# Experts' activations laid out by pairs, fixed tiles, and a new written order for the start of a convolution and gated feed-forward kernel

## The chip, the cores and the metric

The kernel runs on one core of a Trainium2 chip. The metric is the device time of one execution in microseconds (us). TensorE (PE) multiplies matrices, VectorE (DVE) and ScalarE (ACT) work elementwise, GpSimd (POOL) works elementwise and issues the adding DMAs, SyncE (SP) issues the plain DMAs.

## The reference

Sixteen thousand positions (4 sequences of 4160, width 192) pass through two stages.

```
w   = softmax(weight_gen, axis=-1)            # 8 heads x 7 taps a position
y   = sum over k of w[s, head, k] * x[s-6+k]  # each head has 24 of the 192 columns
h   = relu(y @ w_in)                          # 192 -> 1024
c   = conv_w[0]*h[s-1] + conv_w[1]*h[s] + conv_w[2]*h[s+1]
out = (h * sigmoid(c)) @ w_out                # 1024 -> 192
```

## The kernel before

**Tiling.** Each of the 128 partitions holds 130 consecutive positions. They are worked in 33 blocks of 4 positions (R = 4, so 512 columns a block once transposed). Block 0 gives 2 output positions, later ones 4, since the three-tap convolution lags by its edge.

**One block.** POOL multiplies 7 shifted copies of the ring of x with the softmax weights (`tap`, line 324). From block 3 on, two adding DMAs issued by POOL (`fold1`, line 347, and `fold2`, line 350) and one POOL addition (`fold3`, line 357) sum them; in blocks 0 to 2 PE sums them while it transposes (`transposes`, line 372). ACT and DVE split the transposed result into a high and a low part (`split_hi`, 392, `split_lo`, 396). Then follow 8 units, one for each 128 of the 1024 hidden columns (called experts here): `mm1` (5 matmuls, line 410) into one of 5 PSUM tiles z, `relu` (416) from z to h, `wmid` (420) from h to z, two `conv_side` (427), `sig` (434) and `gmul` (472). In blocks 2 to 31 the products of experts 0 and 1 are split once more (`g_hi` 457, `g_lo` 460). `mm2` (493) gives 4 output tiles of 16 matmuls, ACT copies them out (500), POOL adds two halves (506), SP stores (510).

**The carry.** h holds for each expert 6 rows of 128: rows 2 to 5 are the block's, rows 0 and 1 are the last two of the block before. `carry` (line 477) copies rows 4 and 5 to rows 0 and 1 for two experts with one DMA on SP's queue; `relu` of the next block waits for it. In the old layout `h[partition, expert, row, 128]` the two rows of one expert are one piece of 1,024 bytes, so a carry has two pieces a partition.

**Weights.** w_in, conv_w and w_out arrive as 64-bit numbers and are decoded on ACT and DVE in chunks at the start: `shift_exp` (165), `low` (168), `clamp` (172), `shift` (175), `sign` (178), `add` (183), then a split into high and low (687, 692). The chunks of w_in are f0 and f1 (the folded last 64 rows, spread by DMAs from line 706) and m0, m1, m2; conv_w is transposed on PE (658) and read back by ACT (664).

**The order.** Every step is a task with a number, an engine, a duration and its inputs. The instructions are written out in the order of the list `ORDER`, then, for the tasks that are not in it, in the order of a planner that places tasks by these durations and by the arrival times `T_X`, `T_W`, `T_CW` and those in `CH`. Each engine and each DMA queue runs its own instructions strictly in that order. Numbers that are used below: 4 to 11 softmax group 0 (maximum, subtract, exp, sum, epsilon, reciprocal, zero, normalise), 13 to 20 group 1, 22 to 28 group 2, 30 to 36 group 3; 38 to 45 conv_w; 47 to 56 chunk f0, 58 to 65 m0, 67 to 76 f1, 78 to 85 m1, 87 to 94 m2; 129 to 135 the taps k = 0, 1, 2, 4, 5, 6, 3 of block 0, 136 to 153 its transposes and splits, 156 to 162 the taps of block 1; 183 the first `mm1`; 204, 220, 229, 245 the carries of block 0; 288, 304, 320, 336 those of block 1; 338, 435, 536, 638, 740 the loads of x for blocks 3 to 7; 745 the subtract of softmax group 4.

`PLAN` names the engine of each tap of blocks 0 to 2 (V is DVE, G is POOL), in the order k = 0, 1, 2, 3 and then 4, 5, 6 (index i is tap k = i). `SMX` names the engines of a softmax group's subtract and normalise. Where a tap, a subtract or a normalise with both inputs in SBUF runs on DVE (the planner's "VK"), the next POOL instruction in written order is preceded by a token: DVE clears a small tile (`tok`, line 988), and POOL writes it (989), so POOL waits until DVE has come to that place.

**Tiles.** Before, w, the softmax sums, the tap products (px, py), the split inputs and z come from pools that hand out a buffer at each request.

## Time and profile before

| | |
|---|---|
| median of 3 runs | 696.84 us (696.56 to 697.0) |
| profiled execution | 696.19 us, its span 694.5 us |
| PE busy | 674.3 us, 97% of the span |
| DVE busy | 654.7 us, 94% |
| ACT busy | 598.5 us, 86% |
| POOL busy | 570.7 us, 82% |

The span runs from the first to the last instruction of the program in the profile; 1.7 us of the execution lie around it. Busy shares are means over the whole span: the start, in which the weights are decoded and the first blocks are made, and the end differ from the steady part.

### The profile page before, as it was taken

How to read it: one execution, taken by the hardware profiler on the slowest of the kernel's cores; microseconds unless marked ns; L12 is line 12 of the kernel's file. 1: busy time of each engine (PE TensorE's matmuls, PEld its weight loads, DVE VectorE, ACT ScalarE, POOL GpSimd, SP SyncE). 2: the span in 40 equal slices, each digit the busy share in tenths (PEclk: the TensorE clock that was granted, in tenths of full speed). 3: DMA queues.
4: the chain of work that ended last, by engine and by line, in shares of the span. 5: the costliest groups of instructions: out<-in, count | busy, mean ns of one | idle time of the engine just before them, and what ended most of it. 6: DMA issues, size and time to landing. Idle time of an engine off the chain costs nothing.

```text
span 694.5 us, 11226 instructions
## 1 busy us (share of the span) xinstructions
PE 674.3 (97%) x3749; PEld 612.6 (88%) x3749; DVE 654.7 (94%) x1061; ACT 598.5 (86%) x1147; POOL 570.7 (82%) x451
## 2 busy tenths in 40 slices
PE   2999999999999999999999999999999999999998
PEld 2788988999999999999999999999999999999997
DVE  6999998999999999999999999999999999999991
ACT  3778888989898998989899998989899898888982
POOL 5999998899998988989797997989799897971111
PEclk9999999999999999999999999999999999999999
DMA  8627889999899887889788787888878788692211
GB/s 267 205 77 156 216 203 228 211 217 217 201 213 209 176 204 185 210 199 214 198 197 199 174 207 197 205 208 197 202 148 210 179 209 180 159 203 87 83 54 46
DMA packets 70785, 127.61 MB, mean 184 GB/s; under 512 B 5054, under 2 KB 42557, under 8 KB 70728
## 3 DMA queue, kind: packets, MB, share of 16 engines
q0 software_dynamic: 20192, 59.01, 47.1%
q1 hardware_dynamic: 50188, 67.42, 29.2%
q8 instruction: 30, 0.49, 0.3%
q10 hardware_dynamic: 348, 0.47, 0.2%
q14 instruction: 27, 0.22, 0.1%
HBM read 20.51 MB, written 12.78 MB: 48 GB/s over the span
## 4 chain that ended last, share of the span: by engine, by line
PE 84%; POOL 11%; issue 2%; DMA 1%; ACT 1%; DVE 0%; POOLq 0%; ACTq 0%
PE ops L493 43%; PE z L410 38%; POOL px L324 5%; POOL py L324 4%; PE tp L372 3%; DMA h<-h 1%; PE z L493 1%; POOL w L298 0%; POOL w L276 0%; POOL px L350 0%; POOL px L347 0%; POOL px L357 0%; ACT h L416 0%; DVE z L427 0%; ACT z L420 0%
## 5 line engine op out<-in xcount | busy, mean ns | idle before, releaser
L427 DVE SCALAR_TENSOR_TENSOR z<-h,cw,z 128x512 f32<-128x512 f32 (+1 forms) x528 | 376.1, 741 | 8.1 <-ACT z L420 4.4
L410 PE MATMUL z<-H,wi 128*128 128x512 f32 x1056 | 299.1, 404 | 1.9 <-DVE g L472 1.2
L493 PE MATMUL ops<-wo,g 128*128 128x192 f32 x1536 | 273.3, 328 | 0.0
L493 PEld LDWEIGHTS ops<-wo,g 128*128 128x128 f32 x1536 | 246.7, 190 | 0.0
L324 POOL TENSOR_TENSOR px<-ring,w 128x768 f32<-128x768 f32 (+2 forms) x146 | 232.7, 1703 | 1.1
L410 PEld LDWEIGHTS z<-H,wi 128*128 128x128 f32 x1056 | 194.6, 188 | 39.7 <-DVE g L472 2.9
L420 ACT ACTIVATE z<-h,cw 128x512 f32<-128x512 f32 (+1 forms) x264 | 180.0, 682 | 4.8
L324 POOL TENSOR_TENSOR py<-ring,w 128x768 f32<-128x768 f32 (+3 forms) x109 | 170.4, 1912 | 0.0
L434 ACT ACTIVATE z<-z 128x512 f32<-128x512 f32 (+1 forms) x264 | 151.6, 576 | 19.3 <-DVE z L427 14.7
L416 ACT ACTIVATE h<-z 128x512 f32<-128x512 f32 x264 | 155.9, 591 | 10.1 <-PE z L410 7.9
L472 DVE SCALAR_TENSOR_TENSOR g<-z,h 128x512 f32<-128x512 f32 (+1 forms) x198 | 130.6, 675 | 1.2
L506 POOL TENSOR_TENSOR o<-o 128x768 f32<-128x768 f32 x30 | 68.0, 2268 | 48.2 <-ACT o L500 30.9
L410 PE MATMUL z<-L,wi 128*128 128x512 f32 x264 | 103.1, 390 | 0.0
L493 PE MATMUL ops<-wos,gx 128*128 128x384 f32 x480 | 90.5, 310 | 0.5 <-ACT o L500 0.5
L500 ACT ACTIVATE o<-ops 128x384 f32<-128x384 f32 (+1 forms) x128 | 61.5, 483 | 25.6 <-PE ops L493 25.0
L493 PEld LDWEIGHTS ops<-wos,gx 128*128 128x128 f32 x480 | 74.8, 189 | 6.1 <-ACT o L500 0.9
L357 POOL TENSOR_TENSOR px<-px 128x512 f32<-128x512 f32 (+1 forms) x60 | 72.8, 1460 | 3.8 <-DMA px<-px 3.8
L410 PEld LDWEIGHTS z<-L,wi 128*128 128x128 f32 x264 | 49.6, 188 | 11.1
L392 ACT ACTIVATE H<-tp 64x256 fp32r<-64x256 f32 (+1 forms) x93 | 42.5, 458 | 8.7 <-PE tp L372 8.3
L350 POOL DMA_DIRECT2D px<-px x30 | 40.0, 1335 | 11.5 <-DMA px<-py 11.1
L347 POOL DMA_DIRECT2D px<-py x30 | 39.6, 1320 | 9.4 <-POOL py L324 8.2
L472 DVE SCALAR_TENSOR_TENSOR z<-z,h 128x512 f32<-128x512 f32 x60 | 41.7, 695 | 1.3 <-ACT z L434 0.2
(77 smaller groups left out, 384.0 us busy)
## 6 DMA issues: line engine op xcount, KB each, us to landing
px<-py POOLq DMA_DIRECT2D x30, 1152.0 KB, 8.8
h<-h SPq DMA_DIRECT2D x128, 256.0 KB, 4.4
px<-px POOLq DMA_DIRECT2D x30, 768.0 KB, 6.6
ring<-in_x_dram SPq DMA_DIRECT2D x31, 384.0 KB, 5.6
out_dram<-o SPq DMA_DIRECT2D x31, 384.0 KB, 5.7
w<-in_weight_gen_dram SPq DMA_DIRECT2D x15, 224.0 KB, 4.8
r_out<-in_moe_w_out_dram SPq DMA_DIRECT2D x4, 384.0 KB, 4.5
wi<-scr SPq DMA_DIRECT2D x8, 128.0 KB, 3.1
```

The lines of the kernel that those rows point to most:

```text
L324: eng.tensor_tensor(out=dst[:, a:b, :].rearrange("p s (h g) -> p s h g", g=GRP), in0=ring[:, p:p + n, :].rearrange("p s (h g) -> p s h g", ...
L357: nc.gpsimd.tensor_tensor(out=dst.rearrange("p (s d) -> p s d", s=R), in0=a[:, :, lo:hi], in1=b[:, :, lo:hi], op=ALU.add)
L392: nc.scalar.activation(out=hi, in_=src, func=ACTF.Copy)
L410: nc.tensor.matmul(out=z, lhsT=w[:, fs], rhs=h_t[j, nm], start=(i == 0), stop=(i == len(terms) - 1))
L416: nc.scalar.activation(out=hrow(f, 2, R), in_=z_t[j, f], func=ACTF.Relu)
L420: nc.scalar.activation(out=z_t[j, f][:, :no * P], in_=hrow(f, cc, no), func=ACTF.Copy, scale=cw[:, NF + f:NF + f + 1])
L427: nc.vector.scalar_tensor_tensor(out=z, in0=hrow(f, cc + d, no), scalar=cw[:, k * NF + f:k * NF + f + 1], in1=z, op0=ALU.mult, op1=ALU.add,)
L434: nc.scalar.activation(out=z, in_=z, func=ACTF.Tanh, scale=0.5)
L472: nc.vector.scalar_tensor_tensor(out=g_of(j, f), in0=z_t[j, f][:, :no * P], scalar=1.0, in1=hrow(f, cc, no), op0=ALU.add, op1=ALU.mult)
L493: nc.tensor.matmul(out=ps[:, 0:m], lhsT=g, rhs=w, start=(n == 0), stop=(n == len(terms) - 1))
L500: nc.scalar.activation(out=o_t[j][:, 0:n, i, :], in_=ps[:, 0:n * D].rearrange("p (b d) -> p b d", b=n), func=ACTF.Copy, scale=0.5)
L506: eng.tensor_tensor(out=o[:, 0, a:b], in0=o[:, 0, a:b], in1=o[:, 1, a:b], op=ALU.add)
```

## The change

The layout of h becomes `[partition, pair, row, expert of the pair, 128]`. One expert's row is still 128 numbers in a run, but its rows now stand 256 numbers apart, so `relu`, `wmid`, `conv_side` and `gmul` address h as 4 runs of 128. A carry's two rows of two experts are now one piece of 2,048 bytes a partition.

The pools of w, the softmax sums, px, py, the split inputs and z become fixed tiles, as many as before, taken in turn by block or unit number (conv_w takes z tile 0, the units follow from tile 1). The softmax of group 0 subtracts on POOL, that of group 1 subtracts on POOL and normalises on DVE; tap k = 6 of block 0 moves to DVE. The planner's arrival times change, the ring's reuse distance in its model changes from 3 to 4 blocks (`RB`), and `ORDER` is new and has 700 entries instead of 600. The loads at the start are issued as before.

```diff
-    ("a", "GVGGGGG"),
+    ("a", "GVGGGGV"),
...
-SMX = ("VG", "VV", "GG", "GG")
+SMX = ("GG", "GV", "GG", "GG")
...
-T_CW = 3.7
-T_X = (9.0, 12.8, 14.6)
-T_W = (4.2, 11.1, 20.1, 21.1)
+T_CW = 5.0
+T_X = (8.8, 11.0, 12.4)
+T_W = (3.2, 10.0, 16.0, 17.1)
...
-    ("f", 0, 256, 5.3, "VGP", "G"),
-    ("m", 0, 256, 10.1, "VVP", "G"),
-    ("f", 256, 512, 15.7, "GVP", "V"),
-    ("m", 256, 512, 16.8, "VVP", "G"),
-    ("m", 512, 1024, 19.1, "VVP", "V"),
+    ("f", 0, 256, 6.3, "VGP", "G"),
+    ("m", 0, 256, 9.4, "VVP", "G"),
+    ("f", 256, 512, 13.3, "GVP", "V"),
+    ("m", 256, 512, 14.0, "VVP", "G"),
+    ("m", 512, 1024, 15.3, "VVP", "V"),
...
-    "38 40 4 5 47 6 41 39 7 9 49 50 8 10 11 129 42 48 51 52 131 53 130 43 133 132 54 58 44 60 61 59 45 136 137 139 "
-    "141 134 138 13 62 135 140 14 15 142 144 63 64 65 67 16 17 69 70 68 71 72 55 73 74 75 95 18 143 19 78 80 20 156 "
...
+    "38 39 4 5 6 7 9 10 47 8 11 129 49 132 50 40 41 51 131 48 52 53 133 42 54 58 60 61 62 137 59 63 13 14 43 44 64 65 "
+    "68 45 136 55 130 139 67 69 70 71 72 73 22 74 78 75 79 23 135 134 80 15 16 18 81 82 141 143 17 19 83 84 145 138 "
+    "20 338 156 140 142 85 147 144 146 151 148 161 30 152 153 164 149 150 183 157 87 89 90 91 24 163 190 95 197 158 "
...
-    RB = (RING - R - TAPS) // R
+    RB = (RING - R - 2) // R
...
-    h = const.tile([P, NF, R + 2, P], F32, name="h")
+    h = const.tile([P, NF // CG, R + 2, CG, P], F32, name="h")
...
+    px_b = [const.tile([P, 4, R, D], F32, name=f"px{i}") for i in range(NX)]
+    py_b = [const.tile([P, 3, R, D], F32, name=f"py{i}") for i in range(NY)]
+    t_b = [[const.tile([P, W], F32R, name=f"{t}_{i}") for t in ("H1", "L1", "H2")] for i in range(2)]
+    z_b = [ps_z.tile([P, W], F32, name=f"z{i}") for i in range(NZ)]
...
-        z = ps_z.tile([P, W], F32, tag="z", name="z")
-        z_t[j, f] = z
+        z = z_t[j, f] = z_b[(1 + j * NF + (f if j else FORD.index(f))) % NZ]
...
     def hrow(f, a, n):
-        return h[:, f, a:a + n, :].rearrange("p s t -> p (s t)")
+        return h[:, f // CG, a:a + n, f % CG, :]
...
     def carry(f0):
-        nc.sync.dma_start(out=h[:, f0:f0 + CG, 0:2, :], in_=h[:, f0:f0 + CG, R:R + 2, :])
+        nc.sync.dma_start(
+            out=h[:, f0 // CG, 0:2].rearrange("p s f t -> p (s f t)"),
+            in_=h[:, f0 // CG, R:R + 2].rearrange("p s f t -> p (s f t)"),
+        )
```

## Rows read from the trace of the kernel before

**Rows 1.** Windows: stretch, then each engine's busy us and instructions, PE clock, DMA share

```profile
300.00:400.00 100.00, 100.00 (x556) 91.44 (x555) 97.78 (x155) 90.26 (x170) 89.46 (x68) 1.00 0.84 197
```

**Rows 2.** Timeline of PE: start, us, line, operands, count, idle before and its releaser

```profile
23.68 1.17 PE L410 MATMUL z<-H,wi 128*128 128x512 f32 x4
...
29.78 0.96 PE L410 MATMUL z<-H,wi 128*128 128x512 f32 x3 [0.24 <-DVE wi L692]
...
40.29 0.73 PE L410 MATMUL z<-H,wi 128*128 128x512 f32 x2 [0.16 <-DVE H L396]
...
52.26 1.19 PE L410 MATMUL z<-H,wi 128*128 128x512 f32 x4 [0.24 <-DVE gx L472]
...
93.68 0.39 PE L410 MATMUL z<-L,wi 128*128 128x512 f32 x1
94.54 0.81 PE L493 MATMUL ops<-wos,gx 128*128 128x384 f32 x4 [0.47 <-ACT o L500]
...
116.17 0.39 PE L410 MATMUL z<-L,wi 128*128 128x512 f32 x1
117.79 1.21 PE L410 MATMUL z<-H,wi 128*128 128x512 f32 x4 [1.23 <-DVE g L472]
```

**Rows 3.** The chain that ended last, 85 to 150 us: start, us, what

```profile
88.77 0.94 POOL w L276
...
104.88 10.07 DMA h<-h
...
144.44 5.68 PE z L410 x25
```

**Rows 4.** Timeline of POOL

```profile
9.66 1.54 POOL L324 TENSOR_TENSOR px<-ring,w 128x768 f32<-128x768 f32 x1
11.16 2.25 POOL L324 TENSOR_TENSOR px<-ring,w 128x768 f32<-128x768 f32 x1
...
21.58 0.10 POOL L989 MEMSET tok<- 128x1 f32 x1 [1.74 <-DVE tok L988]
...
26.18 0.97 POOL L276 TENSOR_TENSOR w<-w,m 128x448 f32<-128x448 f32 x1
...
62.05 1.54 POOL L324 TENSOR_TENSOR px<-ring,w 128x768 f32<-128x768 f32 x1
```

**Rows 5.** Timeline of SP's queue

```profile
2.54 0.58 SPq L207 DMA_DIRECT2D ring<-in_x_dram  x1
```

**Rows 6.** DMA issues from 0 to 4 us: operands, queue, count, KB, us to landing

```profile
ring<-in_x_dram SPq DMA_DIRECT2D x1, 588.0 KB, 6.2
```

**Rows 7.** Timeline of DVE

```profile
7.61 0.43 DVE L172 TENSOR_SCALAR dps<-dps 128x256 f32<-128x256 f32 x1
...
9.78 2.24 DVE L324 TENSOR_TENSOR px<-ring,w 128x768 f32<-128x768 f32 x1
...
14.69 0.75 DVE L276 TENSOR_TENSOR w<-w,m 128x448 f32<-128x448 f32 x1
...
16.36 0.42 DVE L692 TENSOR_TENSOR wi<-dps,wi 128x256 fp32r<-128x256 f32 x1 [0.57 <-ACT wi L687]
...
22.21 0.68 DVE L396 TENSOR_TENSOR L<-tp,H 128x512 fp32r<-128x512 f32 x1
...
24.32 1.14 DVE L273 TENSOR_REDUCE m<-w 128x64 f32<-128x448 f32 x2
```

**Rows 8.** Timeline of ACT

```profile
6.36 0.40 ACT L165 ACTIVATE dps<-stage 128x256 f32<-128x256 f32 x1 [1.18 <-DMA stage<-in_moe_w_in_dram]
...
66.49 0.58 ACT L416 ACTIVATE h<-z 128x512 f32<-128x512 f32 x1
```

**Rows 9.** The page's DMA queues: packets, MB, share of 16 engines' span

```profile
q0 software_dynamic: 20192, 59.01, 47.1%
q1 hardware_dynamic: 50188, 67.42, 29.2%
```

**Rows 10.** Groups of instructions by shape: count, busy us, mean ns, idle before

```profile
L396 DVE TENSOR_TENSOR H<-tp,H 64x256 fp32r<-64x256 f32 x60 | 25.4, 423 | 7.3 <-ACT H L392 6.3
```

More of the change, by code (lines that the diff above doesn't have):

```diff
@@ L271, in vmax @@
         def vmax():
-            sm_t[j] = [sm_p.tile([P, 2 * R * HEADS, 1], F32, tag=t, name=t) for t in ("m", "r")]
+            sm_t[j] = sm_b[j % 2]
             V.tensor_reduce(out=m(0)[:, :, 0], in_=w(), axis=AX.X, op=ALU.max)
@@ L412, in hrow, with rows @@
     def hrow(f, a, n):
-        return h[:, f, a:a + n, :].rearrange("p s t -> p (s t)")
+        return h[:, f // CG, a:a + n, f % CG, :]
+    def rows(ap):
+        return ap.rearrange("p (s t) -> p s t", t=P)
     def relu(j, f):
-        nc.scalar.activation(out=hrow(f, 2, R), in_=z_t[j, f], func=ACTF.Relu)
+        nc.scalar.activation(out=hrow(f, 2, R), in_=rows(z_t[j, f]), func=ACTF.Relu)
     def wmid(j, f):
@@ L420, in wmid @@
         nc.scalar.activation(
-            out=z_t[j, f][:, :no * P], in_=hrow(f, cc, no), func=ACTF.Copy, scale=cw[:, NF + f:NF + f + 1]
+            out=rows(z_t[j, f][:, :no * P]), in_=hrow(f, cc, no), func=ACTF.Copy, scale=cw[:, NF + f:NF + f + 1]
         )
@@ L425, in conv_side @@
         no, cc = geom(j)
-        z = z_t[j, f][:, :no * P]
+        z = rows(z_t[j, f][:, :no * P])
         nc.vector.scalar_tensor_tensor(
@@ L472, in gmul @@
         nc.vector.scalar_tensor_tensor(
-            out=g_of(j, f), in0=z_t[j, f][:, :no * P], scalar=1.0, in1=hrow(f, cc, no), op0=ALU.add, op1=ALU.mult
+            out=rows(g_of(j, f)), in0=rows(z_t[j, f][:, :no * P]), scalar=1.0, in1=hrow(f, cc, no), op0=ALU.add, op1=ALU.mult
         )
     def carry(f0):
-        nc.sync.dma_start(out=h[:, f0:f0 + CG, 0:2, :], in_=h[:, f0:f0 + CG, R:R + 2, :])
+        nc.sync.dma_start(
+            out=h[:, f0 // CG, 0:2].rearrange("p s f t -> p (s f t)"),
+            in_=h[:, f0 // CG, R:R + 2].rearrange("p s f t -> p (s f t)"),
+        )
     o_t = {}
@@ L558, in load_out @@
             )
-        temps = [hrow(f, 0, R).bitcast(I32) for f in range(2)]
+        temps = [h[:, 1 + i, 0, 0, :].bitcast(I32) for i in range(2)]
         def run(steps):
@@ L629, in bits @@
                     if 0 not in hold:
[L630 removed]
+                        t_ = z_b[0] if own else ps_d.tile([P, W], F32, tag="dps", name="dps")
                         hold[0] = t_.bitcast(I32)[0:t1.shape[0], 0:N]
@@ L742, in loads @@
         def loads(q):
-            if q >= RB:
-                x_t_[q] = dma(1.2, all_taps[q - RB], lambda: load_x(R * q - 1, R * q + 3))
+            if q not in x_t_:
+                x_t_[q] = dma(1.2, all_taps.get(q - RB, []), lambda: load_x(R * q - 1, R * q + 3))
             g = group(q)
```

38 lines of the change are left out of this document (14 added, 24 removed), and 41 rows, old and new, of the table ORDER.

## The prediction, before the result was known

> **What bounds the kernel now.** I read the busy shares by stretch first, then PE's timeline for the places where it stands still, then the chain that ended last, then the timelines of the other engines over the first 25 us. In the steady part PE has no gap at all: 100.00 us busy of 100, with DVE at 97.78, ACT at 90.26 and POOL at 89.46 [rows 1]. Nothing that the change does alters a PE instruction, so a block costs PE the same before and after, and only three things can move the end: when the first unit starts, how often PE stands still after that, and whether another engine becomes slower than PE.
>
> The first unit starts at 23.68 us. After it the reader should look for idle brackets in PE's timeline: there are five that matter, and none after 118 us [rows 2]. Three are small, 0.24, 0.16 and 0.24 us, together 0.64, and DVE releases each. The two large ones I size by spacing, since the ends of matmuls are modelled: 25 matmuls of a unit's kind take 5.68 us where nothing holds them [rows 3], so 0.227 each. From 93.68 to 94.54 is 0.86, less 0.227 makes 0.63 lost; from 116.17 to 117.79 is 1.62, less 0.227 makes 1.39 lost [rows 2]. In all some 2.66 us can be recovered behind the first unit.
>
> The chain tells why the two large ones happen. Up to 88.77 us it runs through POOL without a break, and its last POOL piece there is the subtract of softmax group 4, which DVE's sum and so ACT's copy-out then wait for; the PE gap at 94.54 is its end. The gap at 117.79 hangs on one carry that took 10.07 us to land, issued at 104.88 [rows 3].
>
> **The change part by part.** First POOL, which sets when block 0's products are there. Its first tap starts at 9.66 [rows 4]. The new list does softmax group 0 ahead of the decoding of conv_w, so its normalise no longer holds the tap; the x of block 0 does. That load is issued at 2.54 [rows 5] and takes 6.2 us [rows 6], so the tap can start at 8.8: 0.9 earlier at most. Four taps at a spacing of 1.50 (9.66 to 11.16 [rows 4]) bring POOL to 14.8. A DVE tap in between costs POOL 2.25 less 1.54, 0.71 [rows 4]: 15.5. Then come the two subtracts moved ahead, at 0.97 each as the one that ran alone [rows 4], a second DVE tap at 0.7 to 0.85, and the last POOL tap at 1.50: 15.5 + 1.9 + 0.8 + 1.5 = 19.7. A token stands ahead of the second subtract. DVE comes to tap 1 near 12.9 (it ended chunk m0 at 16.36 + 0.42, less the tap of 2.24, a subtract of 0.75 and an earlier start by 0.9, [rows 7]), has it done near 14.3, and reaches the token after five steps of chunk f1 at 0.42 and a maximum at 0.57: 17.0. POOL is there at 16.5, so 0.5 more: 20.2. Before, POOL was done with block 0 at 21.58 less 1.74, 19.84 [rows 4]. So block 0's last product comes 0.4 later, although POOL begins earlier and has one tap fewer; for that the subtracts of groups 1 and 2 lie behind it.
>
> Now DVE, on which the split of block 0 stands at 22.21 [rows 7]. Removed ahead of it: two subtracts, 0.75 for the larger [rows 7] and by its size some 0.4 for the smaller: 1.15. The first chunk's decoding begins as soon as it has landed, near 6.7, since ACT took it at 6.36 after a wait for the DMA alone [rows 8]; it began at 7.61 [rows 7]: 0.9 earlier. DVE stood idle three times while it waited for ACT, the longest 0.57 [rows 7]; the new list puts other work there, I take 1.0 as gained. Together 3.05. Added ahead of the split: two maxima at 0.57 (1.14 for the pair that now runs after it), two steps of chunk m1 at 0.42, and tap 6. For a DVE tap the only row is 2.24 us [rows 7], of which POOL's own first tap still ran until 11.20 [rows 4]; it ended at 12.02, so 0.82 is its own part and 1.42 was waiting. I take 0.82, because the new place has POOL held at its token; the bounds are 0.82 and 2.24. Added: 1.14 + 0.84 + 0.82 = 2.8. The split so stands at 22.21 - 3.05 + 2.8, about 22.0, and POOL's products plus two transposes and one ACT copy bring it to 22.3. The first unit also waits for a transpose of block 1's first tap, as before, and that tap for the token behind group 1's normalise, which was at 21.58 [rows 4] and moves with DVE by the same 0.2. So the first unit starts at 23.7 as before; the bounds are 0.9 earlier (the whole of the earlier POOL start arrives) and 1.4 later (tap 6 costs DVE 2.24).
>
> The Trainium skill has a rule that speaks against these moves: on the page "SBUF — State Buffer", section "SBUF: two separate sides", DVE instructions with two SBUF inputs and GpSimd instructions exclude each other for a whole instruction, the later one blocking. The rows agree with it, 1.42 us of waiting for DVE and then 0.71 lost on POOL. By the rule tap 6 costs the rest of POOL's running instruction and its own part, by the row's face value 2.24; the sum would be the one above or 1.4 worse.
>
> Second, what is done by then. When the first unit starts, both maxima and the end of m1 lie behind DVE instead of ahead of it (1.14 + 0.84), and no new work of that size has come in: apart from the two subtracts and tap 6 the lists have the same members. So DVE is about 2 us further, less the 0.8 of tap 6 and 0.3 of swaps: 1 us at least. The three small gaps that DVE releases are each 0.24 or less, so a lead of 1 us covers them; I take 0.5 of the 0.64. POOL is ahead by the second subtract.
>
> Third, the gap at 94.54. Softmax group 4's subtract was POOL's 53rd instruction of the list and is its 44th now, some nine instructions or 13 us earlier at 1.5, while DVE's sum for it moves only from the middle of block 3's units to the end of block 2's, one block's quarter. The 0.63 goes. What is next there is ACT's copy-out itself, which has no such wait in front.
>
> Fourth, the carry. 20192 packets of the adding queue take 47.1% of 16 x 694.5 us, 0.259 us each; 50188 of SP's queue take 29.2%, 0.065 each [rows 9]. A carry of 256 pieces has 16 on each DMA engine; taken in turn with the other queue's packets they need 16 x 0.324, 5.2 us, and 8 pieces of twice the size need 8 x (0.259 + 0.065 to 0.13), 2.6 to 3.1. The carry at 104.88 took 10.07, with two adding DMAs in flight, and the new list issues these two about as close. With half the pieces I put it at 5 to 7.5 us. What it cost PE is 1.39, so a landing 2.5 us earlier removes the gap. The bounds are 0 and 1.39.
>
> Fifth, the queues. On SP the load of x for block 7 now stands ahead of three carries of block 1, and it waits for the last tap of block 3, which ended at 62.05 + 1.54, 63.6 [rows 4]. POOL has two taps of later blocks and one of block 0 fewer ahead of it, one subtract and one tap more: 2 us earlier, 61.6. Load and carry are then issued by 63 and land by 65.5; the `relu` that needs the carry ran at 66.49 [rows 8]. So it is hidden by some 1 us; if it is not, ACT waits 1 to 3 us there.
>
> Sixth, edits that I cost at nothing. The fixed tiles are as many as the pools', and the turn is the same as that in which buffers became free. The 4 runs of 128 in h: a DVE split on two strided runs takes 423 ns for 256 numbers [rows 10], one on a single run 0.42 [rows 7], so a run's start shows no price; the cover is DVE's 2.22 us of idle time in 100 [rows 1], which is 18 ns for each of the 24 instructions of a block that read h (5.05 blocks, from 556 matmuls at 110 a block).
>
> **Sum.** Against the profiled execution: 696.19 - 0.5 - 0.63 - 1.39 + 0 = 693.7. The median of the runs shown lies 0.65 above that execution, so the forecast is 694.3.
>
> **Rivals.** *Earlier still:* the 0.9 of POOL's earlier start reaches the first unit. For it speaks that PE only waits for block 0 there; against it the two subtracts put in between. 693.4, down to 692.6 with all small gaps gone.
>
> *The carry's gap stays:* what held it may be the two adding DMAs as such and not its own pieces. 694.3 + 1.39 = 695.7, or more if a copy-out gap comes back. The Trainium skill, page "DMA: Bandwidth & Descriptors", section "Why small descriptors are slow (HBM only)", says that copies inside SBUF don't suffer from small pieces; by it the carry would gain nothing, and this rival holds. No run here shows a carry of larger pieces.
>
> *The load ahead of the carries:* if block 3's last tap doesn't move, load and carry land at 63.6 + 1.3 + 2.4 to 4.4, 67.3 to 69.3, and `relu` waits 0.8 to 2.8. That eats the gain: 695.1 to 697.1.
>
> *DVE's taps lose every turn to POOL (slower):* the row shows DVE let in after one POOL tap. If instead it gets in only when POOL stops at a token, tap 1 waits from 12.9 until POOL's four taps and first subtract are done at 14.8 + 0.97, 2.9 us, and tap 6 waits 2.5 for a subtract and a tap. The first unit is then 5.4 later, 29.1, and the time 694.3 + 5.4 = 699.7. It decides from a first unit at 27.6 on. Against it stand the 2.24 of the row.
>
> *Strided rows cost DVE (slower):* from 18 ns an instruction on DVE is the bound; at 30 ns it is 12 x 24 x 33, 9.5 us: 703.8. The 423 against 420 ns speak against it.
>
> **Chances.** Forecast 0.50, with its own range 693.3 to 695.4; earlier still 0.09; the carry's gap stays 0.16; the load ahead of the carries 0.08; DVE's taps 0.11; strided rows 0.06. A measurement of this kernel can tell 0.2%, 1.4 us: below 695.4 is faster, above 698.2 slower. Faster: 0.48 + 0.09 + 0.03 = 0.60; the same: 0.02 + 0.13 + 0.08 + 0.02 = 0.25; slower: 0.15. The range 692.6 to 697.4 takes in the first four cases, 0.82.
>
> **What would show it.** In the profile after: POOL's first tap near 8.8; the first unit at 22.8 to 25.1; PE's brackets of 30 to 53 us gone or halved; no PE wait for ACT's copy-out near 94; carries that land in under 7.5 us at most and about 3 in the median; `conv_side` as long as before. The forecast is wrong if the first unit starts after 26, if PE has new gaps behind SP's loads near 65, or if PE's steady stretch is below 100%.

## The result and the profile after

The changed kernel takes 700.48 us in the median of 7 runs (698.24 to 701.86); the kernel before, beside it on the same chip, 696.49 (695.24 to 697.0). The ratio is 1.0055, 95% interval 1.0038 to 1.0072: slower by 4.0 us. The forecast was 694.3, with a range of 692.6 to 697.4. The profiled execution took 701.22 us, its span is 699.5, so 5.0 more than that of before.

The steady stretch answers to [rows 1]; columns as there: PE is still without a gap and DVE no busier.

```profile
300.00:400.00 100.00, 100.00 (x555) 91.44 (x554) 97.30 (x154) 90.82 (x173) 90.77 (x71) 1.00 0.85 200
```

PE's timeline, against [rows 2]:

```profile
23.20 0.63 PE L371 MATMUL ops<-ident,px 128*64 128x128 f32 x4 [0.83 <-POOL px L329]
...
25.67 1.06 PE L371 MATMUL ops<-ident,px 128*64 128x128 f32 x4 [1.41 <-POOL px L329]
26.38 2.05 PE L408 MATMUL z<-H,wi 128*128 128x512 f32 x4
...
78.24 1.20 PE L408 MATMUL z<-H,wi 128*128 128x512 f32 x4 [1.81 <-DVE gx L461]
...
140.78 1.20 PE L408 MATMUL z<-H,wi 128*128 128x512 f32 x4 [0.48 <-DVE gx L461]
...
157.40 1.19 PE L408 MATMUL z<-H,wi 128*128 128x512 f32 x4 [0.42 <-DVE gx L461]
```

The first unit starts at 26.38, not 23.68, and its first four matmuls take 2.05 us, not 1.17: behind the waits of 0.83 and 1.41 the granted clock of PE is 0.66 in this stretch (the third number from the end).

```profile
24.00:29.00 5.00, 3.59 (x14) 2.65 (x13) 4.73 (x8) 2.62 (x6) 4.99 (x5) 0.66 0.99 330
```

In five of the changed kernel's seven executions the mean granted clock is 0.995 to 0.998, and these took 699.8 to 701.9 us; the other two, at 0.999 and 1.0, took 698.7 and 698.2, while of 126 executions of the kernel before only seven are below 0.999. So some 2 of the 4.0 us go with a lower clock behind standstills, whatever causes those (an estimate from these seven).

The waits for ACT at 94.54 and for the carry at 117.79 are gone, as forecast. A new wait of 1.81 stands at 78, and DVE releases it. DVE and POOL show why:

```profile
73.89 0.68 DVE L461 TENSOR_TENSOR gx<-z,gx 128x512 fp32r<-128x512 f32 x1
74.49 3.09 DVE L469 TENSOR_TENSOR wos<-wo,wos 128x384 fp32r<-128x384 f32 x1
77.51 0.68 DVE L461 TENSOR_TENSOR gx<-z,gx 128x512 fp32r<-128x512 f32 x1
```

```profile
73.78 1.46 POOL L281 TENSOR_TENSOR w<-w,m 128x448 f32<-128x448 f32 x1
74.71 2.46 POOL L356 TENSOR_TENSOR px<-px 128x512 f32<-128x512 f32 x2
78.87 0.10 POOL L993 MEMSET tok<- 128x1 f32 x1 [1.70 <-DVE tok L992]
```

`wos` is the low part of w_out, a subtraction of two SBUF inputs (task 128; "the split of w_out" below). In the kernel before it took 0.61 us:

```profile
86.89 0.61 DVE L468 TENSOR_TENSOR wos<-wo,wos 128x384 fp32r<-128x384 f32 x1
```

Now it stands next to POOL's subtract and `fold3`, starts at 74.49 and ends, after 3.09 us, 0.42 us behind the last of them (77.17). Everything behind it on DVE is 2.5 us late.

At the start, DVE waits for the weights of softmax group 2, and POOL waits at the token for DVE. DVE's rows begin with its two taps of block 0:

```profile
13.38 1.53 DVE L329 TENSOR_TENSOR px<-ring,w 128x768 f32<-128x768 f32 x1
...
18.98 0.62 DVE L278 TENSOR_REDUCE m<-w 128x64 f32<-128x448 f32 x1 [2.34 <-DMA w<-in_weight_gen_dram]
...
19.86 0.95 DVE L329 TENSOR_TENSOR py<-ring,w 128x768 f32<-128x768 f32 x1
...
23.32 0.61 DVE L303 TENSOR_TENSOR w<-w,r 128x448 f32<-128x448 f32 x1
```

```profile
9.56 1.54 POOL L329 TENSOR_TENSOR px<-ring,w 128x768 f32<-128x768 f32 x1 [1.56 <-DMA ring<-in_x_dram]
...
16.27 0.96 POOL L281 TENSOR_TENSOR w<-w,m 128x448 f32<-128x448 f32 x1
20.02 0.10 POOL L993 MEMSET tok<- 128x1 f32 x1 [2.78 <-DVE tok L992]
20.07 1.57 POOL L281 TENSOR_TENSOR w<-w,m 128x448 f32<-128x448 f32 x1
21.61 1.54 POOL L329 TENSOR_TENSOR px<-ring,w 128x768 f32<-128x768 f32 x1
24.01 0.10 POOL L993 MEMSET tok<- 128x1 f32 x1 [0.87 <-DMA wi<-scr]
24.07 1.55 POOL L329 TENSOR_TENSOR px<-ring,w 128x768 f32<-128x768 f32 x1
```

The chain to the first unit is read from these rows: the load lands at 18.96, DVE's maximum and tap 6 follow, the token at 20.02 lets POOL go on to its subtract and block 0's last tap, and the token at 24.01 (its bracket names a DMA; DVE clears the tile at 23.88, behind its normalise at 23.32) lets POOL start block 1's first tap. PE's transposes of that tap stand right ahead of the first unit.

The page's queues and its row of the carries (count, KB, median us to landing): a third fewer packets on SP's queue, yet the median carry lands in 3.8 us against 4.4 before, and the longest in 9.05 against 10.07 [rows 3, 9].

```profile
q0 software_dynamic: 20192, 59.01, 46.8%
q1 hardware_dynamic: 33804, 67.42, 28.0%
```
```profile
h<-h SPq DMA_DIRECT2D x128, 256.0 KB, 3.8
```

**Where the time goes, along PE.** The matmuls of the first product can be counted in each trace's timeline of PE; the table gives the start of the 1st, 41st, 81st ... of them in the profiled execution before (us), and for every other kernel how much later (+) the same one starts. At 41 and 81 the two lists have transposes and second products at different places, so these two columns compare kernels of one list only. "e" numbers are the experiments below. A minus is a lead. The column "1st" differs by up to 2 us between kernels with the same list, as the loads at the start land differently from one trace to the next.

```
            1st 41st  81st 121st 161st 201st 241st 281st 321st 401st 601st 1001st
before     23.7 39.5  61.2  81.7 102.5 124.2 144.1 164.0 183.9 223.7 323.2 522.1
after      +2.7 +5.1  +2.9  +4.7  +4.5  +3.1  +3.9  +5.0  +5.0  +5.0  +5.0  +5.0
e1         -1.1 -0.9  -0.9  -0.9  -0.8  -2.2  -2.3  -2.3  +0.3  +0.7  +0.7  +0.7
e2         +0.5 +2.3  -0.2  +9.0  +8.6  +7.1  +8.1  +9.2  +9.2  +9.2  +9.2  +9.2
e3         -0.5 +3.4  +1.2  +2.8  +2.6  +1.1  +2.2  +3.2  +3.2  +3.2  +3.2  +3.2
e4         +1.9 +3.6  +1.4  +1.1  +1.0  -0.5  -0.1  +1.2  +1.2  +1.2  +1.2  +1.2
e5         +0.1 +4.8  +2.5  +2.2  +1.9  +0.4  +0.7  +2.1  +2.1  +2.1  +2.1  +2.1
e6         +1.8 +3.6  +1.4  +1.0  +7.3  +5.9  +6.5  +7.6  +7.6  +7.6  +7.6  +7.6
e7         +0.8 +2.6  +0.4  +4.2  +3.9  +2.6  +3.2  +4.2  +4.2  +4.2  +4.2  +4.2
e8         -2.0 -1.8  -1.8  -1.8  -1.9  -3.4  -3.5  -3.5  -0.7  -0.4  -0.4  -0.4
e9         -0.3 -0.1  -0.1  -0.1  -0.2  -1.7  -1.8  -1.8  -1.8  -1.5   0.0   0.0
e10        +2.0 +3.8  +1.6  +1.2  +1.4  -0.1  +0.2  +1.2  +1.6  +1.6  +1.6  +1.6
e11        +1.9 +4.3  +2.1 +10.4 +10.1  +8.6  +9.1  +9.8  +9.8  +9.8  +9.8  +9.8
e13        -1.3 -1.0  -1.0  -1.0  -1.2  -2.7  -2.8  -2.8  -2.8  +1.8  +1.8  +1.8
e16        +0.4 +0.7  +0.7  +0.7  +0.4  -1.1  -1.2  -1.2  -1.2  -0.8  +1.1  +4.3
e18        -1.2 -0.9  -1.0  -1.0  -0.4  -1.9  -1.9  -1.9  -1.2  -0.8  -0.8  +3.3
```

The changed kernel is 2.9 late at the 81st, 1.8 more at the 121st (the gap at 78), 1.4 less at the 201st (the carry's gap gone), and then loses 1.9 by the 281st, of which the gaps at 140.8, 151.9 and 157.4 are 0.65, 0.27 and 0.58 (start to start, less the usual spacing). After that it loses nothing.

### The profile page after: what moved, and what is told of

It reads as the page before. It is cut to its first block, busy times and chain, and to the rows that moved or that the text cites. A ratio compares the mean times of both kernels' runs of the same rounds, so it can differ in the third digit from the quotient of the medians.

```text
span 699.5 us, 11336 instructions
## 1 busy us (share of the span) xinstructions
PE 677.2 (97%) x3749; PEld 613.7 (88%) x3749; DVE 657.8 (94%) x1060; ACT 597.8 (85%) x1147; POOL 570.2 (82%) x452
## 4 chain that ended last, share of the span: by engine, by line
PE 81%; DVE 9%; DMA 3%; ACT 3%; issue 2%; SPq 1%; POOL 0%; DVEq 0%; ACTq 0%
PE ops L497 40%; PE z L408 37%; DVE z L428 5%; PE tp L371 3%; DVE g L473 2%; DMA h<-h 1%; DMA w<-in_weight_gen_dram 1%; DMA ring<-in_x_dram 1%; ACT h L417 1%; ACT z L421 1%; PE z L497 1%; PE ops L371 1%; DVE gx L461 0%; ACT z L435 0%; DVE z L473 0%
## 5 line engine op out<-in xcount | busy, mean ns | idle before, releaser
L329 POOL TENSOR_TENSOR px<-ring,w 128x768 f32<-128x768 f32 (+3 forms) x146 | 224.9, 1730 | 26.8 <-PE tp L371 25.1
L329 POOL TENSOR_TENSOR py<-ring,w 128x768 f32<-128x768 f32 (+2 forms) x108 | 161.2, 1651 | 0.1
```

The costliest lines, as they stand in the source:

```text
L329: eng.tensor_tensor(out=dst[:, a:b, :].rearrange("p s (h g) -> p s h g", g=GRP), in0=ring[:, p:p + n, :].rearrange("p s (h g) -> p s h g", ...
```

## The experiments

Theory: DVE's subtraction of w_out is held by POOL, about 3 us; the late first unit is most of the rest. Rivals: the list as such, the fixed tiles, the layout of h. The kernel before ran beside every group (medians 696.2 to 696.8).

### First, the parts by themselves

**Run 1, e1_old_order.** The changed layout and fixed tiles; list, engines, arrival times and ring distance of before.

```diff
-    ("a", "GVGGGGV"),
+    ("a", "GVGGGGG"),
...
-SMX = ("GG", "GV", "GG", "GG")
+SMX = ("VG", "VV", "GG", "GG")
...
-    "38 39 4 5 6 7 9 10 47 8 11 129 49 132 50 40 41 51 131 48 52 53 133 42 54 58 60 61 62 137 59 63 13 14 43 44 64 65 "
+    "38 40 4 5 47 6 41 39 7 9 49 50 8 10 11 129 42 48 51 52 131 53 130 43 133 132 54 58 44 60 61 59 45 136 137 139 "
...
-    RB = (RING - R - 2) // R
+    RB = (RING - R - TAPS) // R
```

> The changed layout of h and the fixed tiles, with the old list, the old engines and the old arrival times. Theory A (the new list loses the time: DVE stands at softmax group 2's maximum until its load lands, and at the split of w_out while POOL holds the port): as fast as before, 695.0 to 697.0, first unit near 23.7, no DVE wait for a load of w over 0.5. Theory B (the layout or the fixed tiles lose it, by 4 runs of 128 in h or by POOL's new waits for a buffer): 699 to 701, with POOL's waits for PE's transposes near 25 us as in the changed kernel. The forecast's own part on the carry: landing median under 3.9 against 4.4, and the gap of 1.39 gone, so 695.0 rather than 696.5.

697.21 us (ratio 1.0011, interval 1.0002 to 1.0020), just above theory A's range. Layout and tiles alone win nothing and lose almost nothing. The carry's gap is gone (-0.8 to -2.2 from the 161st to the 201st), but the median carry lands in 4.3 us, not in under 3.9, and the 695.0 expected from it didn't come.

**Run 2, e2_new_order_alone.** The new list, engines and times; pools and h as before.

```diff
-        t = w_b[j % WB]
+        t = w_p.tile([P, 2 * R * HEADS, TAPS], F32, tag="w", name="w")
...
-    h = const.tile([P, NF // CG, R + 2, CG, P], F32, name="h")
+    h = const.tile([P, NF, R + 2, P], F32, name="h")
...
```

> The new list, engines and arrival times, with the old layout of h and the pools of before. Theory A: as slow as the changed kernel, 699 to 701, with the DVE wait for group 2's load and the split of w_out at 2.5 to 3.1 us. Theory B: 695 to 697.

705.49 us (1.0131, 1.0118 to 1.0145), above both forecasts. The list is what costs, and with pools twice as much. POOL's timeline has a wait that the changed kernel doesn't have, at a tap that needs a pool's py tile whose last user an adding DMA still reads:

```profile
54.51 1.31 POOL L351 DMA_DIRECT2D px<-py  x1 [0.32 <-POOL px L328]
64.13 1.68 POOL L328 TENSOR_TENSOR py<-ring,w 128x384 f32<-128x384 f32 x2 [8.30 <-DMA px<-py]
```

`fold3` behind it is late, and PE stands 6.07 us at 82; from 81 to 86 us its granted clock is 0.50 (the table: -0.2, then +9.0).

**Run 7, e7_old_h.** The changed kernel with h as before: list and fixed tiles stay.

```diff
-    h = const.tile([P, NF // CG, R + 2, CG, P], F32, name="h")
+    h = const.tile([P, NF, R + 2, P], F32, name="h")
...
-        return h[:, f // CG, a:a + n, f % CG, :]
+        return h[:, f, a:a + n, :]
...
```

> The changed kernel with h as before (a carry is two pieces a partition), fixed tiles and the new list kept. The new list with pools and the old h took 705.5 us. If the fixed tiles alone take that back (a tap that needs a pool's tile waited 8.3 us for the adding DMA that reads the tile's last user), this run is within 0 to 1.4 us of the changed kernel, 700.5 to 701.9 us, and POOL has no wait for an adding DMA at 55 to 65 us. If the layout of h is what takes it back, it stays near 705 us.

700.84 us (1.0067, 1.0052 to 1.0082): as the changed kernel. Here the same tap follows the adding DMA's issue at once:

```profile
54.77 1.31 POOL L346 DMA_DIRECT2D px<-py  x1 [0.31 <-POOL px L329]
55.63 2.18 POOL L329 TENSOR_TENSOR py<-ring,w 128x384 f32<-128x384 f32 x2
```

So the fixed tiles are worth 4.65 us under the new list (705.49 against 700.84, 4.5 by the ratios; apart from the place in h of two scratch areas of conv_w's decoding they are the only difference between these two) and nothing under the old one (run 1 against run 8 below); the layout is worth nothing under the new list. And the carry's gap is gone here too (+3.9 to +2.6 from the 161st to the 201st), with carries of two pieces: the new list alone removes it.

**Run 8, e8_h_alone.** The kernel before with the new layout of h alone; the edit of run 7 the other way round, in the kernel before.

> The kernel before with the new layout of h alone (pools, old list, old engines). If a carry's landing goes with its pieces, and the 10.07 us one cost PE 1.39 us: the longest carry falls to 5 to 7.5 us, the gap near 118 us goes, and the time is 695.4 us. If the adding DMAs in flight set the landing, the longest stays near 9 to 10 us and the time at 696.8 us. If strided rows cost DVE, conv_side is longer than 741 ns and the time above 698 us.

696.82 us (1.0014, 1.0002 to 1.0025). The gap at 118 is gone (-1.9 to -3.4), the strided rows cost nothing, and still the time is no better: the lead goes at 166.7 and 171.6 (-3.5 to -0.7). Of the 3.5 us, 2.0 are an earlier first unit in this trace and 1.5 are the carry's gap. The carry that took 10.07 us takes 8.38 (issued at 102.97, landed at 111.35), the median 4.3 instead of 4.4.

### The split of w_out

**Run 4, e4_split_on_pool.**

```diff
-        nc.vector.tensor_tensor(out=wos[:, :, 1], in0=wo[:, 0:NS], in1=wos[:, :, 0].bitcast(F32), op=ALU.subtract)
+        nc.gpsimd.tensor_tensor(out=wos[:, :, 1], in0=wo[:, 0:NS], in1=wos[:, :, 0].bitcast(F32), op=ALU.subtract)
...
-            return [task("VK", vec(NS * D, 0), [a_], wo_lo)]
+            return [task("G", pool(NS * D), [a_], wo_lo)]
```

> The changed kernel, with the low part of w_out's split computed on POOL in place of DVE, at the same place of the list. Theory A: DVE's 3.09 us at that instruction and PE's gap of 1.97 at 78 us go, 1.5 to 2.0 faster than the changed kernel: 698.5 to 699. If DVE's gap there has another cause (its list is simply late): no change, 700.5.

697.49 us (1.0013, 1.0003 to 1.0023): 0.42%, 2.9 us, better than the changed kernel, and 1 us better than forecast. The gap at 78 is gone; POOL does the subtraction in 1.50. In the two profiled executions PE gains only 2.1 us there (the table, 81st to 121st); 1.5 of the rest lies at the start, which the edit doesn't touch.

**Run 6, e6_split_at_pause.** The subtraction (task 128) stays on DVE and is written 36 entries later.

```diff
-    "395 391 374 375 410 459 128 383 384 419 392 393 396 443 1168 404 405 397 398 543 411 461 542 426 412 413 414 385 "
...
+    "353 395 391 374 375 410 459 383 384 419 392 393 396 443 1168 404 405 397 398 543 411 461 542 426 412 413 414 "
+    "385 447 420 399 400 401 421 422 354 355 356 746 851 427 406 407 128 365 415 462 357 358 359 747 408 409 428 464 "
```

> The changed kernel with the low part of w_out still on DVE, but written 35 entries later, next to the place where POOL issues the second adding DMA of block 4 and so runs no instruction for about 0.8 us. Theory (DVE's instruction with two SBUF inputs is held for as long as POOL runs such instructions back to back): the instruction takes 0.6 to 1.6 us instead of 3.09, PE's gap of 1.97 us near 78 is gone, and the time is 697.5 to 698.5 us. Rival (the stretch has too much work for DVE, and it is the engine that matters, not the place): the instruction may be short, but PE loses as much a little later, and the time stays at 700 to 700.5 us.

703.17 us (1.0102, 1.0088 to 1.0116), worse than either forecast. The subtraction took 0.55 us and the gap at 78 is gone (+1.0 at the 121st), as the theory has it. But the token that follows it held POOL until DVE came there, and `fold3` of block 4 then held PE 3.42 us at 100. Behind that PE's granted clock is 0.50 from 100 to 105 us, and in all 6.3 us are lost by the 161st matmul:

```profile
86.61 0.09 POOL L993 MEMSET tok<- 128x1 f32 x1 [4.13 <-DVE tok L992]
```
```profile
100.41 1.11 PE L371 MATMUL tp<-ident,px 128*128 128x128 f32 x4 [3.26 <-POOL px L356]
```

**Run 10, e10_pause_no_token.** Run 6 with no token behind the subtraction.

```diff
-            return [task("VK", vec(NS * D, 0), [a_], wo_lo)]
+            return [task("V", vec(NS * D, 0), [a_], wo_lo)]
```

> The sixth run (the low part of w_out on DVE, written 35 entries later) without the token behind that instruction. In the sixth run the instruction took 0.55 us, but the token behind it held POOL for 4.13 us, and fold 3 of block 4 then held PE for 3.42 us at 100 us. Theory (the late place is good, the token is what cost): POOL has no wait of 4 us near 82 to 87 us, PE no gap at 100 us, and the time is 697 to 698 us, as with the split on POOL. Rival (POOL's wait was for something else, or fold 3 is late anyway): the gap at 100 us stays at over 2 us and the time at 701 us or more.

697.61 us (1.0024, 1.0009 to 1.0040), 2.9 better than the changed kernel by the medians (2.2 by the ratios, as one of the twelve executions took 703.1), with the subtraction still on DVE. So it is the place, not the engine.

**Run 11, e11_no_token.** The same line changed in the changed kernel itself: old place in its list, no token.

> The changed kernel, the low part of w_out on DVE at its place, without the token behind it, so that POOL goes on with its taps after fold 3 and doesn't stop for DVE. In the changed kernel the instruction took 3.09 us, which is to the end of POOL's fold 3. If DVE gets in only when POOL stops (the prediction's fourth rival): the instruction lasts until POOL's next DMA issue, 5.5 to 7 us in all, and the time is 703 to 704.5 us. If DVE is let in after one or two of POOL's instructions whatever follows: 3.1 us or less, and the time is 699 to 700.5 us, as POOL's wait of 1.7 us is gone.

704.48 us (1.0113, 1.0099 to 1.0128). The subtraction is held for 7.82 us, through POOL's subtract (not shown), both instructions of `fold3` and four taps, until POOL next stops:

```profile
73.67 7.82 DVE L469 TENSOR_TENSOR wos<-wo,wos 128x384 fp32r<-128x384 f32 x1
81.41 0.68 DVE L461 TENSOR_TENSOR gx<-z,gx 128x512 fp32r<-128x512 f32 x1
```
```profile
74.00 2.45 POOL L356 TENSOR_TENSOR px<-px 128x512 f32<-128x512 f32 x2
75.94 2.14 POOL L329 TENSOR_TENSOR px<-ring,w 128x576 f32<-128x576 f32 x2
77.58 3.49 POOL L329 TENSOR_TENSOR py<-ring,w 128x768 f32<-128x768 f32 x2
81.76 1.21 POOL L349 DMA_DIRECT2D px<-px  x1 [0.69 <-DMA px<-py]
```

The subtraction ends at 81.49, 0.43 us behind POOL's last tap (81.06). In all nine traces in which it took over 0.6 us it ended 0.42 or 0.43 us behind the last POOL instruction before a stop (72.89 and 73.31 in run 2, 86.68 and 87.10 in run 18, 87.08 and 87.50 in the kernel before). In the changed kernel the token had ended the wait, by stopping POOL. The fourth rival of the prediction (DVE gets in only when POOL stops) is what happens here, at an instruction that it didn't name.

### The start

**Run 3, e3_max_later.** The maxima of groups 2 and 3 (22, 23) and their subtracts (24, 25) written later.

```diff
-    "68 45 136 55 130 139 67 69 70 71 72 73 22 74 78 75 79 23 135 134 80 15 16 18 81 82 141 143 17 19 83 84 145 138 "
+    "65 68 45 136 55 130 139 67 69 70 71 72 73 74 78 75 79 135 134 80 15 16 18 81 82 141 143 17 19 83 84 145 138 20 "
...
+    "338 156 140 142 85 147 144 146 151 148 161 30 152 153 164 149 150 22 183 157 23 87 89 90 91 163 190 95 197 158 "
```

> The changed kernel, with softmax group 2's maximum behind block 0's splits, and its subtract, exp and sum moved back as much. Theory A: the wait of 2.34 for the load on DVE, the 2.78 that POOL stands at its token and the first matmuls at half rate go; first unit at 23.5 to 24.5, 2.5 to 3.5 faster than the changed kernel: 697.0 to 698.0. If the first unit depends on x or w_in landing late and not on this wait: first unit at 25.5 or later, under 1 us gained.

700.11 us (1.0057, 1.0043 to 1.0071): no gain, though the first unit starts at 23.2, as theory A has it. By the 41st matmul the 3 us are half gone, in two new waits of PE for the weights of a later unit, which ACT and DVE now decode behind the maxima; the subtraction of w_out was held again (2.87).

**Run 5, e5_max_and_split.** Runs 3 and 4 together.

> The changed kernel with both edits together: the maxima of softmax groups 2 and 3 written later (as in the third run) and the low part of w_out on POOL (as in the fourth). If the two costs add up (the split on DVE 2.9 us, the wait for group 2's load 0.4 us), 697.1 us. If the first unit's lateness is paid in full and was only covered in the third run by the split's own wait there (2.87 us for the instruction, 1.74 us of PE), the 2.7 us of the first unit come back here, less the 1.9 us that PE then stood idle at 28 to 30 us: 695.5 to 696.7. If neither matters beyond the engine of the split: 697.5 as in the fourth run.

697.57 us (1.0021, 1.0012 to 1.0029), no better than run 4 alone, and 2.5 better than run 3, from which it differs by the split alone. Run 3's two waits at the start are there:

```profile
29.46 0.50 PE L408 MATMUL z<-H,wi 128*128 128x512 f32 x1 [1.10 <-ACT wi L691]
30.59 0.73 PE L408 MATMUL z<-H,wi 128*128 128x512 f32 x2 [0.62 <-DVE wi L696]
```

**Run 15, e15_old_engines.** Run 10 with `PLAN` and `SMX` of before.

> The tenth run (the changed kernel with the low part of w_out at a place where POOL pauses, no token) with the engines of the kernel before at the start: tap 6 of block 0 on POOL, the subtracts of groups 0 and 1 and the normalise of group 1 on DVE. If the moves between engines are what makes the first 40 matmuls of PE late (3.8 us in the tenth run, of which 1.2 us are left at the 80th), the time is 696.0 to 696.8 us. If it is the new list itself and the later landing of the loads, it stays at 697 to 698 us.

699.75 us (1.0076, 1.0047 to 1.0105), 2.1 slower than run 10 and outside both forecasts; the first unit starts 3.2 later than before instead of 2.0. The nine executions stand in two groups, 698.1 to 699.8 and 704.0 to 705.6, so the size is uncertain, but all are slower than run 10's median. The moves between engines help the new list. That it stays behind is the list's.

### Why a lead doesn't last

In run 8 (layout alone) PE is 3.5 us ahead at the 281st matmul and 0.7 at the 321st. POOL, ACT, DVE and PE, from their timelines:

```profile
163.02 1.46 POOL L276 TENSOR_TENSOR w<-w,m 128x448 f32<-128x448 f32 x1
```
```profile
164.51 0.58 ACT L279 ACTIVATE w<-w 128x448 f32<-128x448 f32 x1 [4.31 <-POOL w L276]
```
```profile
165.99 0.69 DVE L475 SCALAR_TENSOR_TENSOR g<-z,h 128x512 f32<-128x512 f32 x1 [3.46 <-ACT z L437]
```
```profile
166.74 1.19 PE L410 MATMUL z<-H,wi 128*128 128x512 f32 x4 [1.31 <-DVE g L475]
```

The chain is read from the top: softmax group 6's subtract on POOL, its exponential on ACT, the sigmoid behind it, DVE's product, PE. In the kernel before POOL does the same subtract at 163.16, and ACT's wait there is 0.86. POOL came no earlier, so the lead ends at the exponential.

Why POOL came no earlier, its rows tell. Up to 111 us POOL is 1.9 us ahead in run 8, as PE is at the 161st matmul. Then it issues `fold2` twice, each time when `fold1`'s adding DMA has landed; the kernel before, then run 8:

```profile
115.81 1.21 POOL L350 DMA_DIRECT2D px<-px  x1 [2.88 <-DMA px<-py]
...
133.05 1.21 POOL L350 DMA_DIRECT2D px<-px  x1 [1.56 <-DMA px<-py]
```
```profile
114.52 1.21 POOL L350 DMA_DIRECT2D px<-px  x1 [3.51 <-DMA px<-py]
...
132.85 1.21 POOL L350 DMA_DIRECT2D px<-px  x1 [2.69 <-DMA px<-py]
```

The waits are 0.63 and 1.13 us longer, and of POOL's 1.9 us only 0.2 are left. The first of the two adding DMAs flies beside the carry that cost PE its gap. In the four kernels with the old list and the old h (before, runs 12, 14 and 17) this carry takes 9.9 to 10.1 us, the adding DMA 12.5, and POOL's two waits are 2.80 to 2.90 and 1.49 to 1.64; in the six with the old list and the new h (runs 1, 8, 9, 13, 16 and 18) 7.6 to 8.4, 13.1, 3.38 to 3.51 and 2.58 to 2.69. So under the old list the layout takes from POOL, through the adding DMAs, about what it gives PE. Behind the second wait there may be more than the layout: with PE ahead, SP's next carry and load are issued 1.5 and 2.0 us behind that adding DMA, not 3.8 and 4.4.

**Run 9, e9_exp_later**, and its control, **run 12, e12_before_exp** (h as before): exponential, sum and 1e-9 of groups 6 to 9 written later.

```diff
+        seq = head_ + rest
+        for k in range(4):
+            for t_, u_ in ((1172, 906), (1173, 908), (1174, 929)):
+                seq.remove(t_ + 213 * k)
+                seq.insert(seq.index(u_ + 213 * k) + 1, t_ + 213 * k)
...
-        for i in head_ + rest:
+        for i in seq:
```

> The kernel before with the new layout of h, and beside it the exponential, the sum and the 1e-9 of softmax groups 6 to 9 written some seven ACT instructions later (behind the third relu of the next block). With the layout alone PE was 3.5 us ahead of the kernel before at its 280th first-product matmul and 0.7 us ahead at the 320th: there ACT stood 4.3 us at group 6's exponential, which POOL's subtract releases at 164.5 us in both kernels, DVE then 3.5 us behind ACT, PE 1.5 and 1.1 us behind DVE. Theory (what the layout gives back is lost at that written place, to POOL, which is no earlier): ACT no longer stands there, the two gaps at 166.7 and 171.6 us are gone, and the time is 693.3 to 694.5 us. Rival (DVE itself has no more room): the gaps move on by some us, the time stays at 696 to 697 us.

> The kernel before with the same later exponentials of groups 6 to 9 as in the ninth run, h as before. By the theory of the ninth run there is nothing to win: PE has no gap near 166 us in the kernel before, ACT's wait of 0.86 us at the exponential is hidden, and the time is within 0.6 us of the kernel before. If the later exponentials are a gain of their own, this run is as fast as the ninth, 693 to 694.5 us.

Run 9: 696.74 us (1.0006, 0.9997 to 1.0014); run 12: 697.89 (1.0021, 1.0012 to 1.0030). The two gaps are gone and the lead of 1.8 passes the 321st matmul whole, as the theory says. Then 0.40 to 0.42 us goes at each of 223, 263 and 304, and in the control 0.31 to 0.41 at four places: the moved sum and the reciprocal now stand ahead of DVE's split. Both missed their forecasts by that; between the two the new layout is 1.15 us faster.

**Run 13, e13_exp6_later**, and **run 14, e14_before_exp6**: the same for group 6 alone.

```diff
-        for k in range(4):
+        for k in range(1):
```

> The kernel before with the new layout of h and the later exponential, sum and 1e-9 of softmax group 6 alone. In the ninth run, with groups 6 to 9 moved, the give-back at 166 us was gone (PE stayed 1.8 us ahead), and then 0.41 us was lost at each of 223, 263 and 304 us behind groups 7, 8 and 9. Theory (the layout's gain holds if group 6 alone is moved): 1.25 us below the ninth run, 695.2 to 695.6 us, which is faster than the kernel before by about 0.8 us. Rival (group 7's exponential, at its old place, then waits for POOL as group 6's did and takes the lead back at 206 us): 696 to 696.8 us.

> The kernel before with the same three instructions of group 6 moved and h as before. With groups 6 to 9 moved it lost 1.7 us to the kernel before, 0.4 us at each of four places. Theory (it has no lead that could be lost): within 0.6 us of the kernel before, or slower by the 0.3 us of the place behind group 6. The difference to the thirteenth run is what the layout is worth once it is not given back: 1.0 to 1.8 us by the gap at 117.8 us (1.39 us in the kernel before).

Run 13: 699.10 us (1.0030, 1.0018 to 1.0043); run 14: 696.77 (1.0003, 0.9993 to 1.0012). Run 13 is slower than both its forecasts; its rival's mechanism is what happened: group 7's exponential, at its old place, waits 2.91 for POOL at 202, PE then stands 2.39, and its next matmuls run slowly. Timeline of PE, then windows (busy us of PE, PEld, DVE, ACT, POOL, then PE's clock):

```profile
204.53 0.70 PE L410 MATMUL z<-H,wi 128*128 128x512 f32 x2 [2.39 <-ACT z L437]
205.07 0.50 PE L410 MATMUL z<-L,wi 128*128 128x512 f32 x1
205.37 1.91 PE L410 MATMUL z<-H,wi 128*128 128x512 f32 x4
```
```profile
204.00:209.00 5.00, 4.47 (x13) 3.57 (x14) 4.85 (x8) 3.85 (x8) 5.00 (x5) 0.66 0.87 247
209.00:214.00 5.00, 5.00 (x29) 4.55 (x28) 4.55 (x8) 4.70 (x11) 4.95 (x4) 1.00 0.89 188
```

2.8 ahead becomes 1.8 behind. Here the new layout is 2.3 us slower than its control, which has no such wait: POOL does that subtract at 200.78 in run 13, at 199.69 in run 14.

**Run 16, e16_rec_later**, and **run 17, e17_before_rec**: groups 6 to 15 moved, and the reciprocal behind the split.

```diff
-        for k in range(4):
-            for t_, u_ in ((1172, 906), (1173, 908), (1174, 929)):
+        for k in range(10):
+            for t_, u_ in ((1172, 906), (1173, 908), (1174, 929), (1175, 872)):
```

> The ninth run with all softmax groups from 6 to 15 moved (exponential, sum, 1e-9), and the reciprocal written behind the low part of the split, not ahead of it. In the ninth run DVE's split was late by the reciprocal and PE lost 0.41 us behind each of groups 7, 8 and 9; in the thirteenth, group 7's exponential at its old place took 2.6 us and more. Theory (the layout's lead holds where no exponential stands ahead of POOL's subtract): PE has no gap after 100 us and the time is 695.0 to 695.6 us, faster than the kernel before by about 1 us. Rival (POOL's taps themselves are what the lead runs into): a gap behind POOL appears between 200 and 400 us, 696 to 697 us.

> The kernel before with the same moves and h as before. Theory: nothing to keep, within 0.6 us of the kernel before; the difference to the sixteenth run, 1.0 to 1.5 us, is what the layout of h is worth. Rival: the moves are themselves the gain (no difference to the sixteenth run).

701.07 us (1.0067, 1.0053 to 1.0082) and 702.68 (1.0089, 1.0073 to 1.0105): both forecasts missed. The loss moved to the next DVE instruction that PE waits for, at 231.8, 272.2 and so on: 0.56 us each, nine times. Between these two the new layout is 1.6 us faster.

**Run 18, e18_join_behind.** Run 8 with POOL's joins of output halves written behind the subtracts, so that the subtracts come earlier and nothing else moves.

```diff
+        for k in range(10):
+            seq.remove(780 + 213 * k)
+            seq.insert(seq.index(1171 + 213 * k) + 1, 780 + 213 * k)
```

> The kernel before with the new layout of h alone, and on POOL the joins of the output halves written behind, not ahead of, the subtract of softmax groups 6 to 15 (a join held the subtract back by 1.85 us; its result goes to a store that nothing waits for). No DVE, ACT or PE instruction is moved. Theory (the layout's lead is given back because POOL's subtract comes at a fixed time, 163.0 us, and ACT's exponential stands ahead of PE's chain): ACT waits some 1.9 us less at group 6, PE keeps up to 1.4 us of its lead, and the time is 695.0 to 696.0 us against 696.8 us with the layout alone. Rival (the lead is lost to something else on POOL, at the next group at the latest): 696.4 to 697 us, with a gap of the old size near 166 or 206 us.

699.42 us (1.0036, 1.0019 to 1.0053), the twelve runs from 695.25 to 700.63; both forecasts were lower. In the profiled one the lead at the 321st matmul is 1.2 instead of 0.7 and holds until 484; then a join has waited 8.23 us at 445 and held POOL's taps, group 14's exponential waits, and PE loses 4.1 us at once:

```profile
445.49 1.84 POOL L512 TENSOR_TENSOR o<-o 128x768 f32<-128x768 f32 x1 [8.23 <-ACT h L419]
```
```profile
484.58 0.70 PE L410 MATMUL z<-H,wi 128*128 128x512 f32 x2 [2.21 <-ACT z L437]
```

No version that I ran beats the kernel before.

## Why the prediction was wrong

**The step that failed** is "apart from the two subtracts and tap 6 the lists have the same members", from which DVE was put 1 us ahead. The members are the same, but the low part of w_out now has 130 DVE instructions ahead of it, not 154 (tokens not counted), and I priced no instruction by what POOL does beside it except the taps. It costs 2.5 us on DVE in place of nothing, and the time 2.9 by run 4 and 2.5 by run 5 against run 3. With it mended, the changed kernel stands at 697.5, just above the range: this step is not the whole miss. The second is that the sum subtracts recovered gaps as time (below).

**DVE and POOL.** The fourth rival's mechanism was right for another instruction than the one it named, so its 699.7 comes near the 700.48 by luck. The taps got in after one POOL instruction, as in the row of before: tap 1 took 1.53, tap 6 0.95 where POOL stood at its token (I took 0.82). The subtraction of w_out waited for POOL to stop: 3.09, 2.87 and 3.62 us in the changed kernel and runs 3 and 7, 7.82 in run 11, against 0.55 to 0.79 in the kernel before and in eleven runs, where POOL was about to stop or was issuing a DMA (1.61 and 1.18 in runs 2 and 18, where POOL had one or two instructions to go). The Trainium skill, page "SBUF — State Buffer", section "SBUF: two separate sides", says that the first to start holds the port for its whole instruction and the other blocks. The runs agree that DVE blocks; that it blocks for several POOL instructions in a row, and not for one, is what they add. Why taps get in after one isn't settled. The rows differ in two things: the instruction (a tap, whose second input is a repeated weight, against a subtraction), and that POOL's records overlap by 0.05 us at 12 to 16 us and by some 0.5 at 74 to 81.

**The first unit**: 26.38, outside the bounds of 22.8 to 25.1 and past the 26 that I had named as a sign of being wrong. POOL's first tap could start when x was there, but x landed at 9.4, not at 8.8. The maxima were priced at 0.57 each and not with their load, which landed at 18.96 (15.97 before; 16.0 to 19.8 in the runs, whichever list). That took DVE 2.34 and POOL 2.78. In time this shows no price: runs 3 and 5 start PE earlier and gain nothing, since ACT and DVE owe PE the decoded weights right behind. A start that has both in time was not run.

**The gaps.** At 94.54 and 117.79 they went, at 0.63 and 1.39 as summed; small ones stand elsewhere instead (0.36 at 42.9, 0.39 at 89.2). For the first the mechanism was right: POOL's subtract for it came 14.4 us earlier, 73.78 for 88.22. For the carry the changed kernel can't be credited to it: the new list removes the gap with two pieces as well (run 7). Under the old list half the pieces do remove it, but they brought the carry of 10.07 to 8.38 in run 8, not to 5 to 7.5, and the adding DMA beside it landed later, for which the sum has no term. The rival by which the carry gains nothing doesn't hold there either. That strided rows cost nothing was right: `conv_side` took 740 ns against 741. The fixed tiles, put at nothing, save 4.65 us under the new list, where with pools a tap waited 8.30 us for an adding DMA. Whether that is the moment at which a pool gives a buffer back, or another turn of the buffers, these runs don't tell apart.

**The sum itself** took each recovered gap as time. It isn't, shown in run 8: the 1.39 us gap is gone, the time is not better, and the lead ran into POOL's subtract at 163, then (run 13) at 202. Up to 163 us POOL's rows show where its own lead went: 1.7 us to the later landing of two adding DMAs. That POOL's pace is the bound behind that is argued; no run has a faster POOL. The range's lower end doesn't follow from the sum's terms either: 694.3 less 0.9 and the last 0.14 of the small gaps is 693.3, not 692.6. The measured time lies at the other end, so nothing hangs on it.

**Open:** the last 1.2 us or so of the changed kernel with the split mended (697.5 to 697.6 in runs 4, 5 and 10, against 696.2 to 696.8). It isn't the engines (run 15), and run 7 gives no sign that it is the layout. That leaves the new list; the gaps at 41.5 (0.74) and 153.6 (1.24) in run 4 are where PE shows it, and no run takes them apart.

## What to carry to other kernels

When a list is reordered, look for each two-input SBUF instruction of DVE at what POOL runs beside it, and write it where POOL stops for a token or issues a DMA; check whom its own token then holds. A gap that is closed is worth its length only if the engines that feed PE later are ahead as well, so follow the lead from block to block, not from gap to gap. A copy that is made quicker can make another one slower that shares the queues: look at who waits for that one too. And one pair of kernels that differ in one edit is not that edit's price: in five such pairs the new layout of h came out 1.15 and 1.6 us faster (runs 9 and 16), 2.3 slower (run 13), and without effect (run 8 and the changed kernel).
